# Transformer block on one core: regrouping the score-maximum pairs in the projection stage

## The chip, the core and the metric

The kernel runs on one core of a Trainium2 chip. A core has a matrix engine (TensorE, PE in the profile; PEld is its weight load), a vector engine (VectorE, DVE), a scalar engine (ScalarE, ACT), a general engine (GpSimd, POOL) and a queue engine that issues most DMAs (SyncE, SP). Each engine runs its own instructions in the order of the program and waits on semaphores for the others. Matmuls write to PSUM, which VectorE and ScalarE read; everything else lies in SBUF, on chip, or in DRAM.

The metric is device time in microseconds (us) of one launch; lower is better.

## The reference

One transformer block over 2048 tokens of width 640, in float32:

```
h   = x + softmax(q k^T / sqrt(20)) v  @ wo,   q, k, v = layernorm(x) @ wqkv,  32 heads of 20
out = h + (silu(z @ w_gate) * (z @ w_up)) @ w_down,   z = layernorm(h),  1728 hidden columns
```

The softmax subtracts the largest score of each query row. So that row maximum has to be known before the exponentials of the row, and the kernel computes scores twice: once for the maxima, and once for the exponentials.

## The kernel before

The launch has three stages: the projections (layer norm and q, k, v), the attention, and the feed-forward part with the output projection. The change lies in the first.

**Tiling.** The 2048 tokens are four chunks of 512 (`NC`, index c), each of four tiles of 128 (index t). The 32 heads are eight groups of four (`NG`, index g). A unit u = 4g + c is the scores of one group for one chunk of queries. Numbers are split into a high and a low part and multiplied in three products, so a projection block is 15 matmuls: 5 slices of the 640 columns times 3.

**Slots.** The stage is a list of 18 slots per chunk, 72 in all, numbered by `slot[0]`. In chunk 0 they are one slot with two blocks, an empty one, eight slots of a block each (slots 2 to 9), then eight of values. In chunks 1 and 2 there are five key blocks, five query blocks (`query_key`, line 435) and eight values (`value`, line 509: a tile of 128 tokens in two halves of 320 columns). Chunk 3 has the keys, the values, then the queries. The order of emission is the order on each engine.

**What a block leaves behind.** `keep` (lines 468 to 503) empties a block's PSUM tile through ScalarE and VectorE (before slot 8) or ScalarE and GpSimd (after), and for keys of chunks 0 and 1 adds the difference of the two halves of the chunk. The pieces go to DRAM arrays `q_d` and `k_d`, issued by ScalarE one block later (`store`, line 426). The first slots also split the weights into two parts, a slice or more per slot (`split_w`), out of `raw` tiles that the DMA has filled.

**PSUM.** `ps_wide` is a ring of three tiles of two banks, `ps_one` a ring of two tiles of one bank. A block's result lies in half a `ps_wide` tile in early slots and in `ps_one` later. Pairs use `ps_wide`.

**Pairs.** Between the projection matmuls, TensorE computes some of the scores whose row maxima the softmax needs. A pair is two matmuls for one tile of 128 queries against one chunk of 512 keys, two heads at once. There are two kinds:

- `max_pair` (lines 171 to 180) multiplies with the keys themselves; one VectorE reduction over 2 x 512 follows (line 180). It reads `keys[0]` and `queries[0]`, that is, the first unit's operands that the attention stage uses too, loaded by `load_keys` and `load_queries`.
- `max_halves` (lines 183 to 198) multiplies with differences and second halves of the keys. ScalarE writes the positive part of one half (line 193), then VectorE adds the other half and takes the maximum, once per head (line 195). It reads staged operands.

**Staging.** An item is one set of keys or queries for a group and a chunk, loaded into one of four `raw` buffers by four DMAs of SP (`stack`, line 148). The same four buffers hold the weights before. `load_items` loads the next item once its data is stored by plan (`stored_at`) and the pairs that used its buffer are all emitted. `ready` lets a pair go when its two items were loaded two slots earlier or more. This is the planner's count of slots; if a load in fact lands later, TensorE waits for it.

**Lists.** `urgent` holds the first unit's plain pairs with their earliest slots, `early` the staged pairs in a fixed order. `visit(n)` tries to load items and emits up to n pairs, from `urgent` first. It is called inside a block (after 9 of its 15 matmuls, except in chunk 0) with 3, inside a value from slot 10 on with 2, and at the end of each slot with 3 after a block and 2 after a value. The pairs that one visit emits are called a run here.

```
if n == 9 and slot[0] > 9:
    visit(2)
```

All the pairs of this stage are fixed in number; the attention stage computes the remaining maxima.

Of the kernel before, what the change touches and what calls it, by code (L numbers as in the profile page):

```python
# [26 lines left out]
NC = S // CH  # L27
# [3 lines left out]
NG = H // G  # L31
# [13 lines left out]
def tile_block(ctx: ExitStack, tc: tile.TileContext, x, wqkv, wo, wg, wu, wd, out):  # L45
# [27 lines left out]
    def ps_wide():  # L73
        return psum.tile([P, 2, CH], F32, name="ps_wide", tag="ps_wide", bufs=3)

    def ps_one():
        return psum.tile([P, CH], F32, name="ps_one", tag="ps_one", bufs=2)
# [104 lines left out]
    def max_halves(mx, q, k, pair, t, kc):  # L182


        ps = ps_wide()
        for b in range(2):
            rows = slice(b * ROW, b * ROW + NPART)
            nc.tensor.matmul(  # L188
                ps[:, b, :], q[rows, pair, t * P : (t + 1) * P], k[rows, pair, :],
                start=True, stop=True,  # L190
            )
        over = evp.tile([P, 2, CH // 2], F32, name="over", bufs=3)
        nc.scalar.activation(over, ps[:, :, CH // 2 :], AF.Relu)  # L193
        for b in range(2):
            nc.vector.tensor_tensor_reduce(  # L195
                over[:, b], ps[:, b, : CH // 2], over[:, b], 1.0, LOWEST, ALU.add, ALU.max,
                mx[:, b, pair, t, kc : kc + 1],
            )
# [44 lines left out]
    def moved(u, kc):  # L243
        return [t for t in range(TPC) if in_projections(u, kc, t)]
# [23 lines left out]
    with tc.tile_pool(name="pa", bufs=2) as pa:  # L268
# [18 lines left out]
        slot = [0]  # L287
        items, users = [], {}
# [23 lines left out]
        def staged_keys(g, c, kc, k, q):  # L312
            def one(t, pair):
                max_halves(mxs[g * NC + c], items[q][3], items[k][3], pair, t, kc)
                for n in (k, q):
                    users[n] -= 1
                load_items()

            def ready():
                return all(items[n][3] is not None and slot[0] >= items[n][4] + 2 for n in (k, q))  # L320

            pairs = [(t, pair) for t in moved(g * NC + c, kc) for pair in range(2)]
            for n in (k, q):
                users[n] += len(pairs)
            return [(ready, lambda a=a: one(*a)) for a in pairs]

        def unit_keys(u, kc, t, pair):
            max_pair(mxs[u], queries[u], keys[0], pair, t, kc, kc * CH)
            if u == 0 and (kc, t, pair) == (NC - 1, TPC - 1, 1):
                max_all(0)  # L330

        def in_unit(u, kc, at):
            return [
                (lambda: at <= slot[0], lambda t=t, pair=pair: unit_keys(u, kc, t, pair))
                for t in moved(u, kc) for pair in range(2)
            ]

        def staged(g, *sets):

            found = {}  # L340
            for c, kc in sets:
                for which, chunk in ((1, kc), (0, c)):
                    if (which, chunk) not in found:
                        found[which, chunk] = len(items)
                        users[len(items)] = 0
                        items.append([which, g, chunk, None, None])
            return [
                a for c, kc in sets for a in staged_keys(g, c, kc, found[1, kc], found[0, c])
            ]

        urgent = [a for kc in range(NC) for a in in_unit(0, kc, 18 * kc + 7)]
        early = [a for g in range(1, NG) for a in staged(g, (0, 0))]
        early += staged(1, (0, 1)) + staged(2, (0, 1))
        early += [a for g in range(3) for a in staged(g, (1, 1), (1, 0))]
        early += [a for g in range(3, NG) for a in staged(g, (0, 1), (1, 1), (1, 0))]
        early += staged(0, (2, 1), (2, 0))
# [1 line left out]
        def visit(n):  # L358
            load_items()
            for _ in range(n):  # L360
                for queue in (urgent, early):
                    if queue and queue[0][0]():
                        queue.pop(0)[1]()
                        break
# [64 lines left out]
        def query_key(c, m):  # L429

            z_hi, z_lo = zs[c]
            ps = ps_wide()[:, 0, :] if slot[0] < 7 else ps_one()
            for n, (a, w) in enumerate(((z_hi, w_hi), (z_lo, w_hi), (z_hi, w_lo))):
                for k in range(ND):
                    nc.tensor.matmul(  # L435
                        ps, w[:, k, m * P : (m + 1) * P], a[:, k, :],
                        start=(n == 0 and k == 0), stop=(n == 2 and k == ND - 1),
                    )
                    if n == 1 and k == 3 and c:
                        visit(3)  # L440
            keep(c, m, ps)
# [59 lines left out]
        def value(c, t, half):  # L501
            z_hi, z_lo = zs[c]
            ev = evs[t % 2]
            ps = ps_one()[:, :HALF]
            cs = slice(2 * D + half * HALF, 2 * D + (half + 1) * HALF)
            n = 0
            for a, w in ((z_hi, w_hi), (z_hi, w_lo), (z_lo, w_hi)):
                for k in range(ND):
                    nc.tensor.matmul(  # L509
                        ps, a[:, k, t * P : (t + 1) * P], w[:, k, cs],  # L510
                        start=(n == 0), stop=(n == 3 * ND - 1),
                    )
                    n += 1
                    if n == 9 and slot[0] > 9:
                        visit(2)
            dst = ev[:, half * 4 : half * 4 + 4, : G * VW].rearrange("p g (h w) -> p g h w", h=G)
            nc.scalar.activation(
                dst[:, :, :, :DH], ps.rearrange("p (g h d) -> p g h d", g=4, h=G), AF.Copy
            )
            if half == 1:  # L520
                rows = slice((c * TPC + t) * P, (c * TPC + t + 1) * P)
                store((v_d[rows], ev))
            else:
                store()
# [32 lines left out]
        for c in range(NC):  # L557
            lns = []
            work = (some_keys + some_queries if c else first) + parts
            if c == NC - 1:  # L560
                work = some_keys + parts + some_queries

                es[:] = [e for e in es if e is not third]
                es.insert(1, pa.tile([P, ND, CH], F32R, name="z_hi")[:, :2])
            for j, (kind, *which) in enumerate(work):
                slot[0] = 18 * c + j
                if c == 0 and j < 9:
                    for i in range(split_at[j], split_at[j + 1]):
                        split_w(i + 2)
                        if i % 2 == 1 and loaded < 8:  # L570
                            load_w(loaded)
                            loaded += 1
                if j == 0 and c + 1 < NC:
                    if c > 0:
                        load_x(c + 1)
                    lns = norm(c + 1)
                if which:
                    if (c, j) == (0, 0):
                        first_blocks((0, 1), (1, 0), (1, 1), (0, 2), (1, 2))
                        for m, ps in enumerate(firsts):  # L580
                            keep(0, m, ps)
                    else:
                        (query_key if kind == "block" else value)(c, *which)
                visit(2 if kind == "value" else 3)
                finish_keep()
                if c == 0 and j == 6:
                    for ev in evs:
                        nc.gpsimd.memset(ev, 1.0)
                if j == (4 if c == 0 else 3):
                    load_keys(0, slice(c * CH, (c + 1) * CH))  # L590
                if j == (4 if c == 0 else 8) and c < 3:
                    load_queries(c)
                if 0 in ends:
                    finish_at = min(finish_at, slot[0] + 2)
                    if slot[0] == finish_at:
                        max_finish(0)
                if j == 14 and c == 3:
                    load_values(0)
                for _ in range(2 if j >= 5 else 1):
                    if j >= 1 and lns:  # L600
                        lns.pop(0)()
                if c + 1 < NC and 0 <= j - flip_at[c] < ND:
                    flip(c + 1, j - flip_at[c])
                if c == NC - 1 and j == 11:
                    nc.scalar.activation(
                        pa.tile([P, 1], F32, name="exp_table"), eps_t, AF.Exp
                    )
# [418 lines left out]
    for u in range(NU):  # L1026
        g, c = divmod(u, NC)
# [3 lines left out]
        for kt in range(NT):  # L1031
# [51 lines left out]
            k = 2 * (u - NU + 8)  # L1083
# [574 lines left out]
```

## Time and profile before

| | |
|---|---|
| median of 3 runs | 2109.74 us (2107.43 to 2110.51) |
| the profiled execution | 2110.45 us, span 2108.7 us |
| TensorE busy | 2066.6 us, 98% of the span |
| VectorE, ScalarE, GpSimd busy | 79%, 69%, 33% |
| projections | 0 to about 389.5 us of the span |
| attention | about 389.5 to 1980 us |

The span runs from the first to the last instruction. A line of the timeline gives the start and the duration in us, the engine, the line of the kernel, the operation, what it writes and reads, the shape, and how many like it were merged; in brackets the idle time before it and what ended that. In a line of windows stand the stretch, its length, the busy time of TensorE, weight loads, VectorE, ScalarE and GpSimd with their instruction counts, the granted TensorE clock as a share of full speed, the DMA engines' share, and GB/s. A group's line has its busy time and the mean duration of one in ns, then the idle time before. A matmul's end is modelled, so starts tell more than durations.

### The profile page before, as it was taken

The page shows a single profiled execution, that of the slowest core. Times are in us where ns is not written, and L with a number is a line of the kernel's source. Part 1 is how long each engine was busy: PE and PEld are TensorE (multiplying, and loading weights), DVE is VectorE, ACT ScalarE, POOL GpSimd, SP SyncE. Part 2 cuts the span into 40 slices and gives each one's busy share as a digit, 9 for nine tenths or more (in the row PEclk, how much of TensorE's full clock was granted, in tenths as well). Part 3 has the DMA queues.
Part 4 walks back from the last instruction along what each step waited for, and adds up shares of the span by engine and source line. Part 5 has one row for each costly group of instructions (what it writes and reads, how often), then busy time and mean ns, then how long its engine had stood idle before and what let it go on. Part 6 is the DMA issues. An engine that isn't in the chain of part 4 may idle for free.

```text
span 2108.7 us, 37142 instructions
## 1 busy us (share of the span) xinstructions
PE 2066.6 (98%) x12636; PEld 1207.3 (57%) x12636; DVE 1659.5 (79%) x3631; ACT 1445.4 (69%) x2835; POOL 691.2 (33%) x949
## 2 busy tenths in 40 slices
PE   7999999999999999999999999999999999999998
PEld 5656566433333433334333433335578888888888
DVE  6767867788888888888888988886368766666677
ACT  3647575899999999999999999996743222212221
POOL 2231110233443424353420001001135434653555
PEclk9999999999999999999999999999999999999999
DMA  8565544335263443543631213131137755884642
GB/s 257 174 205 179 164 140 127 87 116 153 88 183 103 148 140 118 156 139 133 188 111 56 52 32 94 34 115 61 35 121 266 263 169 188 298 301 159 196 152 94
DMA packets 197285, 305.38 MB, mean 145 GB/s; under 512 B 47440, under 2 KB 82256, under 8 KB 196072
## 3 DMA queue, kind: packets, MB, share of 16 engines
q1 hardware_dynamic: 183512, 274.15, 41.2%
q10 hardware_dynamic: 13584, 28.85, 4.6%
q8 instruction: 102, 1.67, 0.4%
q14 instruction: 87, 0.71, 0.1%
HBM read 203.82 MB, written 98.30 MB: 143 GB/s over the span
## 4 chain that ended last, share of the span: by engine, by line
PE 87%; DVE 6%; DMA 3%; issue 2%; ACT 1%; ACTq 1%; POOL 0%; SPq 0%; DVEq 0%; POOLq 0%
PE acc L960 24%; PE ps_one L950 15%; PE ps_a L1121 15%; PE ps_max L204 12%; PE ps_b L1215 8%; PE ps_one L509 3%; PE ps_wide L188 3%; PE ps_one L435 3%; DVE over L195 2%; PE ps_max L688 2%; DVE mx L180 2%; PE ps_b L688 1%; DMA halves<-j_d 1%; ACTq L426 1%; ACT over L193 0%
## 5 line engine op out<-in xcount | busy, mean ns | idle before, releaser
L956 ACT ACTIVATE probs<-ps_one 128x512 f32<-128x512 f32 x2048 | 1056.9, 616 | 66.1 <-PE ps_one L950 41.3
L210 DVE TENSOR_REDUCE mx<-ps_max 128x1 f32<-128x512 f32 x1472 | 925.6, 683 | 109.3 <-PE ps_one L950 77.6
L950 PE MATMUL ps_one<-q_stk,k_stk 62*128 62x512 f32 x2048 | 586.4, 451 | 2.6 <-DVE m L86 1.7
L960 PE MATMUL acc<-probs,v_stk 128*32 128x512 f32 x4096 | 547.2, 607 | 0.0
L950 PEld LDWEIGHTS ps_one<-q_stk,k_stk 62*128 62x128 f32 x2048 | 251.6, 184 | 432.9 <-ACT probs L956 397.1
L204 PE MATMUL ps_max<-k_stk,q_stk 60*128 60x512 f32 x1472 | 381.7, 425 | 1.4 <-DVE mx L210 1.3
L204 PEld LDWEIGHTS ps_max<-k_stk,q_stk 60*128 60x128 f32 x1472 | 271.9, 186 | 26.6 <-DVE mx L210 2.7
L195 DVE CUSTOM_DVE_ANT_0 over<-ps_wide,over 128x256 f32<-128x256 f32 x512 | 184.7, 420 | 82.9 <-ACT over L193 82.8
L1336 DVE TENSOR_TENSOR tmp<-ps_a,tmp 128x512 f32<-128x512 f32 x208 | 141.2, 689 | 119.9 <-PE ps_a L1121 94.1
L193 ACT ACTIVATE over<-ps_wide 128x512 f32<-128x512 f32 x256 | 138.6, 597 | 76.9 <-PE ps_wide L188 32.2
L1215 PE MATMUL ps_b<-halves,yp 128*128 128x320 f32 x1032 | 179.3, 308 | 2.0 <-DMA halves<-j_d 1.2
L960 PEld LDWEIGHTS acc<-probs,v_stk 128*32 128x32 f32 x4096 | 80.7, 108 | 175.3 <-issue 166.7
L1215 PEld LDWEIGHTS ps_b<-halves,yp 128*128 128x128 f32 x1032 | 165.1, 188 | 18.6 <-POOL yp L86 1.5
L995 POOL TENSOR_TENSOR o<-o,rb 128x512 f32<-128x512 f32 x31 | 39.9, 1286 | 411.2 <-DMA q_stk<-q_d 178.8
L1121 PE MATMUL ps_a<-t,units 128*128 128x512 f32 x624 | 162.6, 396 | 0.0
L1121 PE MATMUL ps_a<-z,units 128*128 128x512 f32 x516 | 133.9, 394 | 0.0
L1121 PEld LDWEIGHTS ps_a<-t,units 128*128 128x128 f32 x624 | 112.6, 188 | 18.8 <-ACT tmp L1349 0.2
L86 POOL TENSOR_TENSOR yp<-y,yp 128x256 fp32r<-128x256 f32 x96 | 60.2, 627 | 188.3 <-ACT yp L85 188.3
L188 PE MATMUL ps_wide<-raw 60*128 60x512 f32 x512 | 107.6, 468 | 12.3 <-DVE mx L195 7.1
L1220 DVE TENSOR_TENSOR h<-ps_b,h 128x320 f32<-128x320 f32 x248 | 109.9, 480 | 6.9 <-PE ps_b L1215 5.4
L1121 PEld LDWEIGHTS ps_a<-z,units 128*128 128x128 f32 x516 | 93.1, 187 | 15.9
L85 ACT ACTIVATE yp<-tmp 128x512 fp32r<-128x512 f32 x40 | 25.3, 632 | 103.1 <-POOL tmp L1208 103.1
(189 smaller groups left out, 2195.5 us busy)
## 6 DMA issues: line engine op xcount, KB each, us to landing
units<-w_d SPq DMA_DIRECT2D x186, 256.0 KB
w_d<-stage SPq DMA_DIRECT2D x106, 256.0 KB
halves<-j_d SPq DMA_DIRECT2D x70, 320.0 KB
j_d<-stage SPq DMA_DIRECT2D x42, 320.0 KB
k_stk<-k_d SPq DMA_DIRECT2D x64, 160.0 KB
q_stk<-q_d SPq DMA_DIRECT2D x64, 160.0 KB
raw<-k_d SPq DMA_DIRECT2D x54, 160.0 KB
rb<-r_d SPq DMA_DIRECT2D x32, 256.0 KB
```

Of the source, the lines that this page charges most:

```text
L188: nc.tensor.matmul(ps[:, b, :], q[rows, pair, t * P : (t + 1) * P], k[rows, pair, :], start=True, stop=True,)
L193: nc.scalar.activation(over, ps[:, :, CH // 2 :], AF.Relu)
L195: nc.vector.tensor_tensor_reduce(over[:, b], ps[:, b, : CH // 2], over[:, b], 1.0, LOWEST, ALU.add, ALU.max, mx[:, b, pair, t, kc : kc + 1],)
L204: nc.tensor.matmul(ps, queries[u][rows, pair, t * P : (t + 1) * P], keys[u // NC][rows, pair, kc * CH : (kc + 1) * CH], start=True, stop=True,
L210: nc.vector.tensor_reduce(mxs[u][:, b, pair, t, kc : kc + 1], ps, axis=AX.X, op=ALU.max)
L950: nc.tensor.matmul(ps, keys[u // NC][rows, p, kt * P : (kt + 1) * P], queries[u][rows, p, :], start=True, stop=True,)
L956: nc.scalar.activation(probs[p][:, b, :], ps, AF.Exp, scale=scale)
L960: nc.tensor.matmul(acc[32 * j : 32 * j + 32, :], values[u // NC][:, kt, j * VW : j * VW + 32], probs[j // 2][:, j % 2, :], start=(kt == 0) ...
L1121: nc.tensor.matmul(ps.rearrange("p (t n) -> p t n", t=TPC), w[k][:, i], z[k][:, :, j], start=(first and m == 0), stop=(last and m == len(n ...
L1215: nc.tensor.matmul(ps, a, b, start=(n == 0), stop=(n == len(pairs) - 1))
L1220: nc.vector.tensor_tensor(out=h, in0=ps, in1=h, op=ALU.add)
L1336: add = lambda out, ps, x: nc.vector.tensor_tensor(out=out, in0=ps, in1=x, op=ALU.add)
```

## The change

There are three edits, all in the projection stage.

Visits: inside a value, only the second half of a tile (the odd value slot) still has a visit of 2 pairs; the visit at the end of a value slot is of 3 instead of 2. Two value slots thus hold runs of 3, 2 and 3 pairs instead of 2, 2, 2 and 2.

First unit: its pairs against key chunks 0 and 1 leave `urgent` (and with it `max_pair`) and go to the front of their places in `early`, so they are done by `max_halves` with staged operands. This makes 272 staged pairs and 16 plain ones out of 256 and 32, and 54 items out of 50. The first two items are now loaded in slot 4, ahead of the loads of `keys[0]` and `queries[0]` in that slot. Before slot 24, `ready` asks for three slots since the load instead of two.

Wide tiles: a block's result lies in `ps_wide` up to slot 4 instead of slot 6; slots 5 and 6 now use `ps_one`.

```
             def ready():
-                return all(items[n][3] is not None and slot[0] >= items[n][4] + 2 for n in (k, q))
+                return all(items[n][3] is not None and slot[0] >= items[n][4] + 2 + (slot[0] < 24) for n in (k, q))
...
-        urgent = [a for kc in range(NC) for a in in_unit(0, kc, 18 * kc + 7)]
-        early = [a for g in range(1, NG) for a in staged(g, (0, 0))]
-        early += staged(1, (0, 1)) + staged(2, (0, 1))
+        urgent = [a for kc in (2, 3) for a in in_unit(0, kc, 18 * kc + 7)]
+        early = [a for g in range(NG) for a in staged(g, (0, 0))]
+        early += [a for g in range(3) for a in staged(g, (0, 1))]
...
-            ps = ps_wide()[:, 0, :] if slot[0] < 7 else ps_one()
+            ps = ps_wide()[:, 0, :] if slot[0] < 5 else ps_one()
...
-                    if n == 9 and slot[0] > 9:
+                    if n == 9 and half and slot[0] > 9:
                         visit(2)
...
-                visit(2 if kind == "value" else 3)
+                visit(3)
```

## The prediction

> **What bounds the kernel now.** I read the page first, then busy time by stage, then TensorE's waits in the stage that the change touches, then the order of instructions there.
>
> ```profile
> span 2108.7 us, 37142 instructions
> PE 2066.6 (98%) x12636; PEld 1207.3 (57%) x12636; DVE 1659.5 (79%) x3631; ACT 1445.4 (69%) x2835; POOL 691.2 (33%) x949
> ```
> ```profile
> 0.00:389.50 389.50, 361.29 (x1773) 247.42 (x1773) 281.22 (x1210) 228.01 (x420) 79.29 (x66) 0.98 0.58 175
> 48.40:55.20 6.80, 6.33 (x15) 4.74 (x16) 5.45 (x10) 2.38 (x4) 2.10 (x3) 0.50 0.96 293
> 120.10:126.90 6.80, 5.95 (x17) 3.58 (x17) 2.15 (x12) 2.17 (x4) 1.74 (x2) 0.50 0.63 212
> ```
>
> TensorE (first column after the length, then weight loads, VectorE, ScalarE, GpSimd, clock, DMA share) is busy throughout; the edit lies wholly in the projections, which the first stretch holds, and leaves the rest of the kernel alone, so I assume that what the projections save or lose goes through to the end. There TensorE has 389.5 - 361.3 = 28.2 us without a matmul, and its busy time also holds hidden costs: switches between kinds of matmul, and 2 x 6.8 us at half clock (0.50 in the last two rows). Those three are all that can be won; the number of matmuls does not change.
>
> **Part 1: fewer runs among the values.** A run is a few pairs of score matmuls (L188 or L176) between projection matmuls (L509 values, L435 blocks). Its price shows in the starts:
>
> ```profile
> 279.06 0.73 PE L188 MATMUL ps_wide<-raw 60*128 60x512 f32 x4
> 279.72 0.42 PE L509 MATMUL ps_one<-w_lo,z_hi 128*128 128x320 f32 x1
> 279.97 0.89 PE L509 MATMUL ps_one<-w_hi,z_lo 128*128 128x320 f32 x5
> 280.80 0.85 PE L188 MATMUL ps_wide<-raw 60*128 60x512 f32 x4
> 281.58 0.66 PE L405 MATMUL ps_one<-ident,xt 128*128 128x128 f32 x4
> ```
> ```profile
> 195.46 1.08 PE L435 MATMUL ps_one<-z_lo,w_hi 128*128 128x512 f32 x4
> 196.47 0.96 PE L188 MATMUL ps_wide<-raw 60*128 60x512 f32 x6
> 197.37 0.50 PE L435 MATMUL ps_one<-z_lo,w_hi 128*128 128x512 f32 x1
> ...
> 198.95 0.85 PE L188 MATMUL ps_wide<-raw 60*128 60x512 f32 x4
> 200.00 0.50 PE L188 MATMUL ps_wide<-raw 60*128 60x512 f32 x2 [0.19 <-DVE mx L195]
> 200.43 1.43 PE L435 MATMUL ps_one<-z_hi,w_hi 128*128 128x512 f32 x5
> ```
> ```profile
> 131.36 1.30 PE L435 MATMUL ps_one<-z_hi,w_hi 128*128 128x512 f32 x5
> 132.50 1.30 PE L435 MATMUL ps_one<-z_lo,w_hi 128*128 128x512 f32 x5
> ```
>
> Two pairs take 279.72 - 279.06 = 0.66 us and three 197.37 - 196.47 = 0.90, so a pair is 0.24 and a run adds 0.66 - 0.48 = 0.18 of its own. Undisturbed, five block matmuls take 132.50 - 131.36 = 1.14; the six between two runs take 198.95 - 197.37 = 1.58 where 6/5 x 1.14 = 1.37 would do: 0.21 more for leaving and coming back. A run removed saves about 0.18 + 0.21 = 0.39 us.
>
> Followed slot by slot, the two lists hold the same 288 pairs before and after, in 119 and 106 runs: among the values 64 runs become 48 (two slots had four runs of 2, and get 3, then 2 and 3), among the blocks 55 become 58. That is 16 x 0.39 = 6.2 saved, and 3 x 0.39 = 1.2 lost.
>
> Against it stands PSUM. There are three wide tiles. The run at 196.47 filled all three, and its third came back for the pair at 200.00, 3.53 us after the run's start. VectorE's reductions follow each other at 0.35 us, two to a pair:
>
> ```profile
> 268.63 0.42 DVE L195 CUSTOM_DVE_ANT_0 over<-ps_wide,over 128x256 f32<-128x256 f32 x1 [0.25 <-ACT over L193]
> 268.98 0.08 DVE L195 DVE_READ_ACCUMULATOR2_ANT mx<- 128x1 f32 x1
> 268.98 0.42 DVE L195 CUSTOM_DVE_ANT_0 over<-ps_wide,over 128x256 f32<-128x256 f32 x1
> ```
>
> So tiles come back 0.70 apart, the first two at about 2.13 and 2.83. After the change, the run of 3 that ends an odd value slot starts 0.66 + 1.08 = 1.74 us after the run of 2 inside it (279.06 to 280.80). Its second pair, due at 1.98, waits for the first tile of the run of 2 until 2.13; its third, then due at 2.37, waits until 2.83: 0.61 us in all. The run of 3 after a whole value finds its tiles free. Before, two end runs pay 281.58 - 280.80 - 0.66 = 0.12 each. So a pair of slots nets 0.39 - (0.61 - 0.24) = 0.02 by this pessimistic count, and 0.39 if the tiles return in time. I take 0.2, between the two, because VectorE's return times were read where it also had other work: 16 x 0.2 = **3 us saved**, ends 0.3 and 6.2. Blocks: **1.2 lost**, ends 0 and 1.2.
>
> [...]
>
> **Part 2: three slots' notice before slot 24.** The longest stall after the start is a load that arrives late in slot 21:
>
> ```profile
> 115.99 1.07 PE L435 MATMUL ps_one<-z_lo,w_hi 128*128 128x512 f32 x4
> 118.45 0.46 PE L188 MATMUL ps_wide<-raw 60*128 60x512 f32 x1 [1.39 <-DMA raw<-q_d]
> 120.95 1.61 PE L188 MATMUL ps_wide<-raw 60*128 60x512 f32 x5 [2.04 <-DMA raw<-q_d]
> 122.50 0.79 PE L435 MATMUL ps_one<-z_lo,w_hi 128*128 128x512 f32 x1
> 123.09 2.33 PE L435 MATMUL ps_one<-z_hi,w_lo 128*128 128x512 f32 x5
> 125.36 1.65 PE L188 MATMUL ps_wide<-raw 60*128 60x512 f32 x6
> ```
>
> Four matmuls take 1.01 (195.46 to 196.47), so the run was due at 117.00: 1.45 late. The run then takes 122.50 - 118.45 = 4.05 instead of 0.90, and the six matmuls after it 2.86 instead of 1.58 (197.37 to 198.95), since the clock is at 0.50 from 120.10. Together 1.45 + 3.15 + 1.28 = 5.9 us. The pairs that waited (group 7) were loaded in slot 19; in the new lists they are loaded in slot 19 too, but used from slot 22. Slot 20 keeps 6 pairs, so this is one slot of at least 4.4 us more against 3.5 us of waiting: **5.9 saved**.
>
> Late next: first unit's key differences for chunk 1, loaded in slot 22, used in slot 24, and group 1's, loaded in 23, used in 25. SP issues them behind the key load of slot 21. The late load's own history sets the margin: issue from 113.21 for 3.10 us (below), last landing 120.95, some 4.6 us after the last issue. Two slots are about 10.7 us, two loads of the kind need 7 to 11. I book **1 lost**, ends 0 and 5.9.
>
> **Part 3: first unit's chunks 0 and 1.** 16 pairs leave the plain reduction for the halved one:
>
> ```profile
> L193 ACT ACTIVATE over<-ps_wide 128x512 f32<-128x512 f32 x256 | 138.6, 597 | 76.9 <-PE ps_wide L188 32.2
> ```
> ```profile
> 142.76 1.01 PE L176 MATMUL ps_wide<-k_stk,q_stk 60*128 60x512 f32 x4
> 144.41 0.49 PE L176 MATMUL ps_wide<-k_stk,q_stk 60*128 60x512 f32 x2 [0.63 <-DVE mx L180]
> 144.83 1.43 PE L435 MATMUL ps_one<-z_hi,w_hi 128*128 128x512 f32 x5
> ```
>
> ScalarE gains 16 x 0.597 = 9.6 us, inside its 389.5 - 228.0 = 161 us of idle. TensorE's part is equal. A run of 3 plain pairs took 144.83 - 142.76 = 2.07 against 1.48 for halved ones (198.95 to 200.43): 0.6. In chunk 1 about two runs are so: **1.2 saved**, ends 0 and 1.8. Four more loads (54 for 50) give 16 more issues on SP; it idles between them, unless loads pile up as below.
>
> **Part 4: the start, slots 4 to 9.** The part I know least.
>
> ```profile
> 37.25 0.74 ACT L85 ACTIVATE w_hi<-raw 128x640 fp32r<-128x640 f32 x1 [3.49 <-DMA k_stk<-k_d]
> 43.09 0.77 PE L176 MATMUL ps_wide<-k_stk,q_stk 60*128 60x512 f32 x2
> 45.66 0.51 PE L176 MATMUL ps_wide<-k_stk,q_stk 60*128 60x512 f32 x2 [1.81 <-DVE v_stk L86]
> 48.87 0.80 PE L176 MATMUL ps_wide<-k_stk,q_stk 60*128 60x512 f32 x2 [2.70 <-DVE e L476]
> 49.59 2.50 PE L435 MATMUL ps_one<-z_hi,w_hi 128*128 128x512 f32 x5
> 55.85 0.97 PE L176 MATMUL ps_wide<-k_stk,q_stk 60*128 60x512 f32 x6
> ```
> ```profile
> 45.03 3.84 SPq L148 DMA_DIRECT2D raw<-q_d  x4
> 113.21 3.10 SPq L148 DMA_DIRECT2D raw<-q_d  x4
> ```
>
> Now the slot-7 pairs wait for slots 5 and 6 to be emptied from wide tiles: 49.59 - 43.09 = 6.50 instead of 0.90, 5.6 lost; and slot 8's block runs at half clock. With the change slots 5 and 6 go to the two ps_one tiles. The pairs find wide tiles free, but slot 7's own block now needs slot 5's tile, which VectorE released just before 45.66; so the same emptying is waited for earlier. And the pairs need two staged loads. The second reuses the weight buffer whose last split (slot 5) freed the query load at 45.03; it lands about 45.03 + 3.84 + 4.6 = 53.5. Should nothing move earlier, the three pairs start at 53.5 instead of ending by 49.59: 53.5 + 0.9 - 49.6 = 4.8 lost. What moves earlier: ScalarE stood 3.49 us behind the landing of the first unit's key load. That load and the query load now go behind the staged ones, so evacuation and splits may run 3.5 us sooner, or more; then 1.3 is lost, and the half clock, which costs slot 8 55.85 - 49.59 - 3.4 = 2.9, may go. So -4.5 to +4.8; I take **0**, the middle. Behind SP's waiting load stand the key, query and group 1 loads; group 1's pairs in slot 9 wait for the latter. That cost lies within the range.
>
> [...]
>
> **Sum.** -3 + 1.2 - 5.9 + 1 - 1.2 + 0 = -7.9 us. The profiled execution took 2110.45 us (span 2108.7), 0.7 above the median 2109.74: 2110.45 - 7.9 = 2102.6, or 2102 against the median.
>
> **Rivals.**
> *The start gets clean*: ScalarE, free of the key load's landing, empties early, no half clock: 4.5 better, 2097.5. For it: the 3.49 us row. Against it: two loads must land where none was waited for.
> [...]
> *The late load only moves* to slots 24 and 25, half clock included: 5.9 instead of 1, 2107.5.
> *Slower: first unit's staged load holds the start.* SP is in order; if stores of ScalarE must wait for the key and query loads stuck behind the 45.03 load, as they waited 3.49 us before, evacuation of slots 6 to 8 stops until they land. Two more batches of four at 3.1 to 3.8 us plus 4.6 after 48.87 give 60 to 61, against 49.59: 11 lost there, and 4.8 more as group 1's load slips likewise: 2102.5 + 15 = 2118. It decides once slot 8 starts 12 us late. For it: the 3.49 row shows the coupling; against: that row's load goes.
>
> **How the numbers follow.** Forecast 0.52, clean start 0.19: faster 0.71. Full PSUM 0.08 and moved load 0.08 end within 0.2% (4.2 us, about what a measurement of this kernel tells from no change): same 0.16. Held start: slower 0.13. Range 2094 to 2110: from a clean start with part of the larger run saving to the two that end level; the held start is left out.
>
> **What would show it.** Right: values' runs at 48, no DMA wait before 118 to 121, clock 0.50 there gone, L176 x32 instead of x64. Wrong: a gap over 4 us before the first L188, a wait on raw near 130, third pairs at over 0.6 us of wait, or a change after 389 us that isn't the shift.

## The result, and the profile after

| | median | range | runs |
|---|---|---|---|
| before | 2108.98 us | 2106.56 to 2112.41 | 12 |
| after | 2109.83 us | 2106.14 to 2114.71 | 12 |

The ratio of after to before is 1.0005, with a 95% interval of 0.9996 to 1.0014: no difference that these runs can tell. The forecast was 2102 us and faster. The profiled execution of after took 2110.56 us. Its page and its projections:

```profile
PE 2063.7 (98%) x12636; PEld 1209.8 (57%) x12636; DVE 1652.8 (78%) x3679; ACT 1451.7 (69%) x2851; POOL 691.3 (33%) x949
```
```profile
0.00:391.90 391.90, 358.58 (x1773) 247.77 (x1773) 275.43 (x1258) 234.50 (x435) 79.25 (x66) 0.99 0.58 179
```

TensorE's busy time in the projections fell by 361.29 - 358.58 = 2.7 us, yet the projections end 2.4 us later, so TensorE stands idle 5.1 us longer. I cut the stage at the first matmul of each kind of work (B: blocks, V: values; the number is the chunk). Windows of after, columns as before (length, busy time of TensorE and the others, clock, DMA share):

```profile
22.95:65.34 42.39, 33.89 (x141) 25.20 (x139) 27.58 (x81) 18.93 (x36) 7.10 (x8) 0.95 0.83 250
65.34:101.34 36.00, 35.44 (x203) 27.18 (x203) 23.77 (x120) 26.42 (x50) 7.75 (x6) 0.92 0.53 163
...
326.67:363.24 36.57, 32.75 (x188) 23.76 (x186) 26.96 (x107) 17.67 (x37) 1.28 (x1) 1.00 0.38 116
```

| stage | before | after | b4 (below) |
|---|---|---|---|
| B0, from the first block | 38.68 | 42.39 | 35.81 |
| V0 | 36.46 | 36.00 | 33.57 |
| B1 | 60.74 | 59.91 | 56.11 |
| V1 | 35.73 | 34.94 | 34.70 |
| B2 | 64.42 | 63.94 | 62.25 |
| V2 | 35.98 | 36.30 | 34.30 |
| keys of chunk 3 | 31.20 | 30.24 | 30.08 |
| V3 | 34.22 | 36.57 | 33.51 |
| queries of chunk 3 | 29.51 | 28.69 | 28.35 |
| sum | 366.94 | 368.98 | 348.68 |

Each column is one execution. The start lost 3.7 us, V3 lost 2.4, and everything else gained 4.0 together, half of what was forecast. The first block starts within 1.9 us of the same time in all kernels here; I compare sums from there. TensorE's waits in the projections, first of before, then of after (engine, what it waited to do, for whom; us in total, times, longest):

```profile
PE ps_wide L188 <- DVE mx L195: 7.1, 24, 0.9
PE ps_wide L188 <- DMA raw<-q_d: 3.4, 2, 2.0
```
```profile
PE ps_wide L188 <- DVE mx L195: 11.4, 40, 1.2
PE ps_wide L188 <- DMA raw<-q_d: 7.5, 7, 2.6
PE ps_one L435 <- DVE v_stk L86: 2.3, 1, 2.3
```

The load wait at 118 to 121 us is gone, as forecast. In its place come a start that waits for loads and pairs that wait for wide tiles. The prediction's signs of being wrong show as well: waits for a wide tile reach 1.2 us (it named 0.6 for third pairs), and a staged load is waited for 0.8 us at 137.79 (it named 130). The start first (TensorE's timeline of after, then SP's):

```profile
46.57 0.47 PE L188 MATMUL ps_wide<-raw 60*128 60x512 f32 x1 [0.42 <-DMA raw<-q_d]
49.60 0.93 PE L188 MATMUL ps_wide<-raw 60*128 60x512 f32 x5 [2.56 <-DMA raw<-q_d]
50.46 2.21 PE L435 MATMUL ps_one<-z_hi,w_hi 128*128 128x512 f32 x5
...
60.21 0.73 PE L188 MATMUL ps_wide<-raw 60*128 60x512 f32 x4
63.31 0.47 PE L188 MATMUL ps_wide<-raw 60*128 60x512 f32 x1 [2.36 <-DMA raw<-q_d]
64.64 0.76 PE L188 MATMUL ps_wide<-raw 60*128 60x512 f32 x1 [0.87 <-DMA raw<-q_d]
65.34 1.70 PE L509 MATMUL ps_one<-w_hi,z_hi 128*128 128x320 f32 x5
```
```profile
41.79 3.66 SPq L148 DMA_DIRECT2D raw<-q_d  x4
45.55 2.38 SPq L148 DMA_DIRECT2D k_stk<-k_d  x4
49.48 4.15 SPq L148 DMA_DIRECT2D q_stk<-q_d  x4
53.73 4.28 SPq L148 DMA_DIRECT2D raw<-k_d  x4
58.11 3.88 SPq L148 DMA_DIRECT2D raw<-q_d  x4
```

Slot 8's block starts at 50.46, 0.9 us later than before. The loss is one slot further on: group 1's queries, wanted at 60.9, are issued from 58.11 only, behind two loads (45.55 and 49.48) that in this kernel nothing reads before slot 43. Behind the wait the granted clock is 0.50 from 64.48 to 71.30, so the clock of V0 reads 0.92.

### The profile page after: what moved, and what is told of

The parts are those of the page before. It is cut to its first block, busy times and chain, and to the rows that moved or that the text cites. A ratio compares the mean times of both kernels' runs of the same rounds, so it can differ in the third digit from the quotient of the medians.

```text
span 2108.8 us, 37276 instructions
## 1 busy us (share of the span) xinstructions
PE 2063.7 (98%) x12636; PEld 1209.8 (57%) x12636; DVE 1652.8 (78%) x3679; ACT 1451.7 (69%) x2851; POOL 691.3 (33%) x949
## 4 chain that ended last, share of the span: by engine, by line
PE 84%; DMA 4%; DVE 4%; issue 3%; ACT 1%; POOL 1%; SPq 1%; ACTq 0%; POOLq 0%; DVEq 0%
PE acc L960 24%; PE ps_one L950 15%; PE ps_a L1121 15%; PE ps_max L204 12%; PE ps_b L1215 8%; DVE over L195 2%; PE ps_one L509 2%; PE ps_one L435 2%; PE ps_max L688 2%; PE ps_wide L188 2%; PE ps_b L688 1%; DMA halves<-j_d 1%; ACT over L193 1%; DMA raw<-k_d 1%; DMA k_d<-v_stk 1%
## 5 line engine op out<-in xcount | busy, mean ns | idle before, releaser
L195 DVE CUSTOM_DVE_ANT_0 over<-ps_wide,over 128x256 f32<-128x256 f32 x544 | 195.3, 420 | 97.9 <-ACT over L193 97.8
L193 ACT ACTIVATE over<-ps_wide 128x512 f32<-128x512 f32 x272 | 145.8, 598 | 73.2 <-PE ps_wide L188 31.3
L1215 PEld LDWEIGHTS ps_b<-halves,yp 128*128 128x128 f32 x1032 | 165.2, 188 | 18.4 <-POOL yp L86 1.5
L188 PE MATMUL ps_wide<-raw 60*128 60x512 f32 x544 | 111.3, 462 | 20.4 <-DVE mx L195 11.4
```

The costliest lines, as they stand in the source:

```text
L188: nc.tensor.matmul(ps[:, b, :], q[rows, pair, t * P : (t + 1) * P], k[rows, pair, :], start=True, stop=True,)
L195: nc.vector.tensor_tensor_reduce(over[:, b], ps[:, b, : CH // 2], over[:, b], 1.0, LOWEST, ALU.add, ALU.max, mx[:, b, pair, t, kc : kc + 1],)
L1215: nc.tensor.matmul(ps, a, b, start=(n == 0), stop=(n == len(pairs) - 1))
```

## Experiments

All ratios below are to runs of before on the same chip, with 95% intervals. The stage lengths and their sums are from one profiled execution each. They differ by up to 2.0 us between kernels that run the same code there (B0 is 42.39 in after and 40.39 in `a3_unit`), and a profiled execution can lie some us off its kernel's median (`a1_notice` 4.0 below; `a5_runs_notice`, `b1_late` and `b2_pool` 4.2, 5.2 and 5.4 above). So they show where time goes, and the ratios decide how much. First I took the change apart.

**One: the notice alone** (`a1_notice`).

```diff
-  return all(... slot[0] >= items[n][4] + 2 for n in (k, q))
+  return all(... slot[0] >= items[n][4] + 2 + (slot[0] < 24) for n in (k, q))
```

> The kernel before with one edit: before slot 24 a unit's pairs become ready three slots after its loads were issued instead of two. Theory 1 (each gain is real and the new start eats them): the load wait and the half clock at 118 to 121 us go, the projections end at 383 to 385 us instead of 389.5, the time falls by 4 to 6 us. Theory 2 (the late load and the half clock only move to another place): half a clock for at least 3.4 us at a new place in the projections, their end within 1.5 us of 389.5, the time unchanged. Theory 3 (what the projections save is lost again behind them): the projections end near 384 and the time is still unchanged.

Measured: 2109.04 us, ratio 1.0004 (0.9995 to 1.0013). The sum from the first block is 365.63, only 1.3 below before. No load was waited for at 118, but there was a stall in the same slot, with half a clock behind it. Timeline of all engines, then two windows:

```profile
112.09 2.53 ACTq L426 DMA_DIRECT2D k_d<-e  x3
114.75 1.57 ACT L193 ACTIVATE over<-ps_wide 128x512 f32<-128x512 f32 x3 [3.66 <-DMA k_d<-e]
115.38 0.42 DVE L195 CUSTOM_DVE_ANT_0 over<-ps_wide,over 128x256 f32<-128x256 f32 x1 [4.12 <-ACT over L193]
116.30 0.50 PE L188 MATMUL ps_wide<-raw 60*128 60x512 f32 x2 [2.11 <-DVE mx L195]
```
```profile
111.54:114.96 3.42, 2.66 (x11) 1.66 (x11) 0.00 (x0) 0.21 (x1) 0.35 (x1) 1.00 0.83 276
114.96:118.37 3.41, 1.88 (x8) 1.24 (x9) 2.96 (x15) 3.18 (x6) 1.24 (x1) 1.00 0.77 257
118.37:121.79 3.42, 3.42 (x10) 2.65 (x9) 2.54 (x12) 1.34 (x2) 1.33 (x2) 0.50 0.62 170
```

Read it from the top: ScalarE issues three stores of keys and stands 2.53 us at them. It evicts the wide tiles (L193) only behind them, at 114.75. VectorE waits 4.12 us for that, and TensorE 2.11 us for a free tile. None of my theories had this wait; theory 2 is nearest.

**Two: the runs alone** (`a2_runs`).

```diff
-                    if n == 9 and slot[0] > 9:
+                    if n == 9 and half and slot[0] > 9:
...
-                visit(2 if kind == "value" else 3)
+                visit(3)
```

> The kernel before with the two edits on runs alone: three pairs instead of two in a run behind a value slot, and no run inside an unsplit half. Theory 1: 13 to 16 runs fewer by some 0.39 us each, less the wide-tile waits of the third pairs: projections end 2 to 4 us earlier than 389.5, time 2 to 4 us lower, the wait and the half clock near 120 us still there (perhaps a slot away). Theory 2 (the third pair of each run waits for its PSUM tile and takes the gain): stages of values as long as before within 0.5 us each, time within 1 us. If the first value slots of a chunk lose time to ScalarE, which stands at its own k_d and q_d stores, chunk 3's values are about 2 us longer here too.

Measured: 2108.68 us, ratio 0.9999 (0.9988 to 1.0011). Sum 365.71, 1.2 below before. V0, V1 and V2 are 1.1, 0.2 and 0.3 shorter, V3 is 36.23, 2.0 longer, as the third sentence said. TensorE still waits 2.5 us for loads between 108 and 130 us, with half a clock for 3.4 us from 119.67.

**Three: everything but the runs** (`a3_unit`: the changed kernel without the second experiment's edit).

> The changed kernel with the runs among values as before: three slots' notice, the first unit staged with the key differences, wide tiles for five slots only. Theory 1: the stage to slot 10 is about 4 us longer than before's 61.3 us with a half clock near 64 us, the wait at 118 to 121 is gone, so projections end at 388 to 391 us and the time is within 2 us of before. Theory 2: the same start, and a new load wait with half a clock behind slot 21: projections end at 393 us or later, time 2 to 4 us above before.

Measured: 2110.22 us, ratio 1.0007 (0.9996 to 1.0019). First value at 64.09 and half a clock from 64.96 to 68.38, as in after; B0 40.39, sum 370.53. The projections end at 394.23, as theory 2 has it, though no wait for a staged load is over 1.9 us. The four stages of values take 143.26 us here and 143.81 in after: in the changed kernel the larger runs gave nothing.

**Four: notice and runs, old start** (`a5_runs_notice`: experiments one and two together).

> The changed kernel with the first unit and the wide tiles as before: fewer, larger runs among values and the three slots' notice. Theory 1: start as before (first value at 61.3 us), no half clock between 65 and 200 us, projections end at 381 to 386 us, time 4 to 8 us lower: the start alone is what the changed kernel loses by. Theory 2: the larger runs wait where the smaller did not and the load wait moves: projections end at 388 to 391 us, time within 2 us of before. Theory 3: projections end near 384 us and the time does not follow.

Measured: 2106.92 us, ratio 0.9994 (0.9985 to 1.0004). The start is before's, first value at 60.12, but the sum is 368.28: V3 took 38.00 us, and half a clock stands at 117.81 and at 332.86. So the old start doesn't bring the forecast gain back, and theory 1 falls as well. The same stall as in the first experiment stands at both places. In after it can be seen at the start of V3, on ScalarE and on TensorE:

```profile
325.94 2.57 ACTq L426 DMA_DIRECT2D k_d<-e  x3
328.63 1.57 ACT L193 ACTIVATE over<-ps_wide 128x512 f32<-128x512 f32 x3 [2.15 <-DMA k_d<-e]
```
```profile
326.11 0.62 PE L188 MATMUL ps_wide<-raw 60*128 60x512 f32 x3
...
330.18 0.50 PE L188 MATMUL ps_wide<-raw 60*128 60x512 f32 x2 [1.05 <-DVE mx L195]
```

A run of three fills all three tiles; while ScalarE stands at its stores, 2.57 us here, none comes back. The new theory: ScalarE's stores hold the projections, in both kernels (the hold, below). SP's rows in the projections after 60 us hint at the coupling of the two queues. In after:

```profile
SPq L148 <- DMA v_d<-ev: 16.0, 5, 5.8
SPq L148 <- DMA q_d<-e: 10.5, 5, 3.5
...
SPq L148 <- DMA k_d<-e: 9.0, 8, 3.2
```

SP's loads at line 148 read `q_d` and `k_d`, yet wait 16.0 us for the landing of stores to `v_d`, which they don't read. The instructions in the trace of after name a completion semaphore for each transfer: the 1587 transfers of SP and the 109 of ScalarE name the same eight. In each of the five waits of these 16.0 us (5.8, 5.2, 0.4, 0.4 and 4.3), the semaphore waited for is the one that SP's next issue names. It goes the other way too: in before, ScalarE's stores of keys at 116.92 and 118.04 are issued 0.02 us after the landings of SP's loads `raw<-k_d` and `raw<-q_d` that had the same semaphores. So here a load of SP waited for the landing of a store of ScalarE, and a store for that of a load. Two edits follow: other loads at the start, and another engine for the stores.

**Five: the two unread loads later** (`b1_late`).

```diff
-                if j == (4 if c == 0 else 3):
+                if j == (11 if c == 0 else 3):
                     load_keys(0, slice(c * CH, (c + 1) * CH))
-                if j == (4 if c == 0 else 8) and c < 3:
+                if j == (12 if c == 0 else 8) and c < 3:
                     load_queries(c)
```

> The changed kernel with the loads of chunk 0's k_stk and q_stk, which nothing reads before slot 43 now, issued behind slots 11 and 12 instead of slot 4. If group 1's query load is late in slot 9 because it queues behind them on SP, the matrix unit's wait for raw at 61 to 65 us is gone, the first value starts at 60.5 to 62 us instead of 65.3, there is no half clock near 64 us, and the projections end 3 to 5 us earlier. If the load is late for another cause (the stores it reads, or the buffers), the first value stays at 64 to 66 us.

Measured: 2114.12 us, ratio 1.0027 (1.0014 to 1.0040). The first value starts at 62.09, 39.20 after the first block, against 42.39 in after; the wait in slot 9 and the half clock at 64 are gone. The cause of that wait is settled. But V0 takes 45.01 us, and the kernel is slower than before. The next loads are late again. Little of that is the moved loads' own issue (3.1 us on SP, from 81.89); most of it is SP waiting for stores of `v_d`, before the moved loads and within the issue at 88.96 (SP's waits from 62.09 to 107.10, then SP's and TensorE's timeline):

```profile
SPq L148 <- DMA v_d<-ev: 11.4, 2, 6.2
```
```profile
88.96 7.52 SPq L148 DMA_DIRECT2D raw<-q_d  x4
```
```profile
95.09 0.46 PE L188 MATMUL ps_wide<-raw 60*128 60x512 f32 x1 [2.57 <-DMA raw<-q_d]
99.25 1.61 PE L188 MATMUL ps_wide<-raw 60*128 60x512 f32 x5 [3.71 <-DMA raw<-q_d]
```

**Six: GpSimd issues the stores of the changed kernel** (`b2_pool`).

```diff
-        def store(*last, queue=nc.scalar):
+        def store(*last, queue=nc.gpsimd):
...
-            store(*pieces, queue=nc.sync if (c, m) == (NC - 1, 2 * ND - 1) else nc.scalar)
+            store(*pieces, queue=nc.sync if (c, m) == (NC - 1, 2 * ND - 1) else nc.gpsimd)
```

> The changed kernel with the stores of k_d, q_d and v_d in the projections issued by GpSimd instead of ScalarE. If ScalarE, held at its own stores, holds the evictions of the wide tiles and with them the matrix unit, then the matrix unit's waits of ps_wide for mx (11.4 us, 40 of them) fall to 2 to 5 us, chunk 3's values return from 36.6 to about 34.5 us, and the projections end 4 to 8 us earlier, unless GpSimd, which splits the blocks, is late with its splits then. If the third pair's own place in PSUM makes those waits, they stay at 10 to 12 us and the projections end within 1.5 us of before.

Measured: 2095.96 us, ratio 0.9949 (0.9930 to 0.9968). Waits of TensorE, then of SP, in the projections:

```profile
PE ps_wide L188 <- DMA raw<-q_d: 7.7, 5, 3.6
PE ps_wide L188 <- DVE mx L195: 5.6, 29, 0.3
```
```profile
SPq L148 <- DMA k_d<-e: 4.3, 1, 4.3
```

The waits for wide tiles halve and none is over 0.3 us; SP no longer waits for `v_d` at all; V3 is 33.50. What is left of load waits, 7.7 us, lies mainly at the start, which is as long as in after (42.05). A store keeps GpSimd busy for 0.51 to 0.69 us; that is hidden (GpSimd is busy 133 of the 349 us in b4's stages).

**Seven: both** (`b4_pool_late`: edits five and six in the changed kernel).

> Both edits together (chunk 0's k_stk and q_stk loaded behind slots 11 and 12, stores issued by GpSimd). If the start and ScalarE's stores are two separate losses, their gains add: projections end at 380 to 385 us, time 7 to 11 us below the changed kernel's. If one stall only covers the other, the gain is that of the better of the two alone.

Measured: 2090.17 us against 2108.53 of before on that chip, ratio 0.9918 (0.9903 to 0.9933). This beats both kernels. The projections end at 371.17, and their sum is 20.3 us below after's, where edit six alone took off 8.9 and edit five alone added 10.3 (by the ratios about 18 and 12 us off and 5 added). So the two don't add: the late loads that cost V0 so much beside ScalarE's stores cost nothing here. In the rows shown SP issues four transfers in 1.5 and 2.3 us, where after took 2.4 to 4.3. SP's start, and TensorE's waits:

```profile
41.02 2.28 SPq L148 DMA_DIRECT2D raw<-q_d  x4
46.67 1.48 SPq L148 DMA_DIRECT2D raw<-k_d  x4
```
```profile
PE ps_wide L188 <- DVE mx L195: 5.6, 29, 0.3
...
PE ps_wide L188 <- DMA raw<-q_d: 1.6, 3, 0.8
```

**Eight: notice, runs, old start, GpSimd's stores** (`b5_runs_pool`: experiment four with edit six).

> The kernel before with fewer, larger runs among values, three slots' notice, and the stores issued by GpSimd; first unit and start as before. If ScalarE's k_d store is what stands behind the load wait at 111 to 117 us, the gap of 2 to 3 us there and the half clock behind it are gone, and the projections end at 380 to 385 us. If the half clock comes at a fixed 71.7 us after the first one whatever the gaps, it stays at 117 to 120 us.

Measured: 2094.30 us, ratio 0.9939 (0.9924 to 0.9953). Sum 350.85, and at full clock from 50.30 to the end of the stage: here neither the gap nor the half clock at 118 comes. In before it had begun 71.7 us after the first one (48.43 and 120.11); here the first one comes too, and none begins 71.7 us later.

**Nine: the kernel before with GpSimd's stores, none of the change** (`c1_before_pool`).

> The kernel before with one edit: GpSimd issues the stores of k_d, q_d and v_d in the projections. If ScalarE's stores held the matrix unit in the kernel before as in the changed one, and the change's own edits come to little, this kernel is 10 to 14 us below before (2095 to 2099, projections end at 375 to 380 us) although none of the change is in it. If ScalarE's hold matters only where the changed kernel's larger runs meet it, the time falls by less than 5 us.

Measured: 2096.22 us, ratio 0.9935 (0.9921 to 0.9948), sum 354.06. So the stores cost the kernel before as much, 12.9 us in the trace. The late load at 118 that Part 2 of the prediction was about is gone too, without any notice. Before issued its keys from 109.72 and its queries from 113.21; here:

```profile
105.71 2.39 SPq L148 DMA_DIRECT2D raw<-k_d  x4
108.20 2.14 SPq L148 DMA_DIRECT2D raw<-q_d  x4
```

With this base I could weigh the change's parts free of the hold.

**Ten: b4 without the larger runs** (`c2_no_runs`).

> The changed kernel with GpSimd's stores and chunk 0's k_stk and q_stk loaded late, but the runs among values as before. With the hold gone the larger runs should save what was worked out for them, 3 us between 0.3 and 6.2: so this kernel ends its projections 1 to 5 us later than the 371.2 us of the same kernel with larger runs, in the four stages of values (33.6, 34.7, 34.4 and 33.5 us there). Under the rival, that the third pair of a run waits for its PSUM tile and eats the gain whoever stores, the stages of values are within 0.3 us each of those.

Measured: 2094.86 us, ratio 0.9935 (0.9917 to 0.9953); the interval overlaps b4's. Sum 350.72, 2.0 above b4's 348.68. V0 to V3 were 35.04, 34.23, 35.13 and 33.18, 1.5 longer together.

**Eleven: b4 with two slots' notice** (`c3_no_notice`).

> The changed kernel with GpSimd's stores and late loads of chunk 0's k_stk and q_stk, but two slots' notice throughout. If the notice is worth what was worked out for it, a wait for raw of 3 to 4 us comes back near slots 20 to 22 with a half clock behind it, and the projections end 4 to 6 us later than 371.2. If loads are late only because their issue was held by the semaphores that SP shared with ScalarE's stores, they land within two slots now and the projections end within 1.5 us of 371.2.

Measured: 2107.67 us, ratio 0.9992 (0.9982 to 1.0002). Neither expectation: nothing came back near slot 21, but the start took 52.38 us instead of 35.81, with waits of 5.30, 3.66, 3.55 and 1.93 us for staged queries between 45 and 69 us. The notice is what makes the new start possible; it isn't a gain on its own.

**Twelve: b4 with wide tiles for seven slots** (`c4_wide7`).

> The changed kernel with GpSimd's stores and late loads of chunk 0's k_stk and q_stk, but wide tiles for the first seven slots. The wait of slot 7's block for the tile of slot 5's (2.0 us) goes; if nothing else takes its place the first value starts at 56 to 57.5 us instead of 58.3 and the projections end 1 to 2 us earlier. If that wait only hides ScalarE's or VectorE's lag, the start is as long as with five.

Measured: 2094.73 us, ratio 0.9931 (0.9915 to 0.9946), overlapping b4's. The wait of slot 7's block goes, but the start takes 37.81 us, 2.0 more than b4's: the first pairs wait 2.24 us for a wide tile that VectorE has yet to empty, then 2.00 for a load. As the prediction had it, the same emptying is waited for at one place or the other. The sum is 354.47, so 3.8 us more are lost behind the start, where this edit changes nothing; why is open.

Two things were still open: whether it is ScalarE that should not issue, or SP that waits, and whether the notice by itself is worth anything.

**Thirteen: SP issues the stores of the changed kernel** (`b3_sync`: as in experiment six, with `nc.sync`).

> The changed kernel with the projections' stores issued by SP instead of ScalarE; loads, start and runs as changed. Two things can be behind the gain of GpSimd's stores. If it is ScalarE alone, which no longer stands at its stores when a wide tile is to be evicted, this kernel gains the same 12 to 14 us (2095 to 2098; waits of ps_wide for mx near 5.6 us). If it is SP, whose loads waited for the landing of stores, the stores in its own order hold the loads as much or more: the waits for mx fall to about 6 us, the waits for raw stay at 7 us or grow, and the time stays within 3 us of the changed kernel or above it.

Measured: 2097.79 us, ratio 0.9948 (0.9933 to 0.9962); TensorE no longer waits for any staged load, though SP itself waits 34.2 us for GpSimd's splits before its stores. The waits for wide tiles are 7.3 us, above the 5.6 expected. Here SP's loads stand between stores in one queue, and the gain is that of GpSimd's stores (0.9949), so that alone isn't the loss. The loss is with ScalarE as issuer. Whether all of it is ScalarE's own standing, or part of it loads that came late because ScalarE's store was late, these runs don't separate: without ScalarE's stores both go.

**Fourteen: notice alone on the kernel of experiment nine** (`d1_notice_pool`).

> The kernel before with GpSimd's stores and the three slots' notice. Without the notice the same kernel took 0.9935 of before and its matrix unit waited 0.4 us for raw. If the late load at 118 us was itself made by ScalarE's stores, the notice has nothing left to save: ratio within 0.002 of 0.9935, projections end within 1.5 us of 377.1 us. If the notice is worth its 4 to 6 us whoever stores, the projections end at 371 to 373 us.

Measured: 2096.36 us, ratio 0.9943 (0.9930 to 0.9955); sum 353.97 against 354.06. The notice saves nothing once ScalarE doesn't store.

## Why the prediction was wrong

**What bounds.** That the projections' gain goes through to the end held: b4's stages are 366.94 - 348.68 = 18.3 us shorter, its time 18.4 us. But the view was incomplete. The gaps were counted on TensorE alone; the waits of ScalarE and SP, which show who held the tiles and the loads, weren't read by cause.

**Part 2 is the first step that failed:** "one slot of at least 4.4 us more against 3.5 us of waiting: 5.9 saved", with 1 us for what is late next. By itself the notice moved the sum by -1.3 us, where -4.9 was booked, and the time not at all (experiment one). Behind the late load stood ScalarE's store of keys in the same slot: the same place, the same half clock, another releaser. Before's trace has both, the store and what made the load late (ScalarE's and SP's timelines, then a row of SP's waits from 28 to 130 us):

```profile
115.12 3.23 ACTq L426 DMA_DIRECT2D k_d<-e  x3
```
```profile
109.72 3.44 SPq L148 DMA_DIRECT2D raw<-k_d  x4
```
```profile
SPq L148 <- DMA v_d<-ev: 5.0, 1, 5.0
```

ScalarE stands 3.23 us at its stores, to 118.35; TensorE waits for the load from 117.06. And the load was late because SP stood from 104.66 to 109.66 for the landing of a store of `v_d` by ScalarE; without ScalarE's stores that wait and the late load are gone (experiments nine and fourteen). I asked what is late next among loads only, and not among the engines that free the tiles.

**Part 1 failed too: the price was right, its cover wasn't.** A run of three behind a run of two:

```profile
175.61 0.73 PE L188 MATMUL ps_wide<-raw 60*128 60x512 f32 x4
...
177.35 0.88 PE L188 MATMUL ps_wide<-raw 60*128 60x512 f32 x4
178.43 0.50 PE L188 MATMUL ps_wide<-raw 60*128 60x512 f32 x2 [0.19 <-DVE mx L195]
178.86 0.66 PE L405 MATMUL ps_one<-ident,xt 128*128 128x128 f32 x4
```

It takes 178.86 - 177.35 = 1.51 instead of 0.90: 0.61, the number of the prediction. Free of the hold the values went from 139.47 to 136.58 us (`d1_notice_pool` to `b5_runs_pool`), 2.9 saved where 3 was forecast, and the blocks lost 0.0 of the 1.2. But experiment ten has 1.5 for the same edit, the ratios tell neither from nothing (0.9943 and 0.9939, 0.9935 and 0.9918, with overlapping intervals), and a price of 0.61 goes with the prediction's pessimistic end of 0.3. So that 2.9 lies so near to 3 may be luck. With ScalarE's stores the same edit gave 141.89 to 144.68 (`a1_notice` to `a5_runs_notice`), 2.8 lost, all in V3, and 0.5 lost in the changed kernel. The working took ScalarE as free because it idles 161 us; a run of three needs it free just then: the run of two before it started 1.74 us earlier (175.61 to 177.35).

**Part 3.** The plain pairs' matmuls went from 64 to 32, as said. No run isolates the 1.2 us. The four more loads weren't free: the staged pairs at the start wait 0.42 and 2.56 us for theirs, which belongs to Part 4.

**Part 4: 0 booked, +3.7 measured** (+1.7 in `a3_unit`, with the same start), within its ends of -4.5 and +4.8; half a clock (0.50, 64.48 to 71.30) then stands over the start of V0. The better end isn't worked out there: 1.3 lost less 2.9 for the half clock is -1.6, and no row gives the rest. The pieces came as written: ScalarE's row that stood at 37.25 starts at 35.22, slot 7's block waits 2.3 us for slot 5's tile, and the first staged pairs wait until 49.60. The sentence on group 1's load, "that cost lies within the range", was the part that happened: 2.36 and 0.87 us of waiting, behind loads that nothing reads soon (experiment five).

**The sum.** Forecast -7.9. In the trace of after: +3.7 at the start, -1.7 in all later stages, where -7.9 had been expected: +2.0. The times say +0.9, within what they can tell. Of the 9.9 us between, the start makes 3.7, the stages of values 4.4 (+1.4 instead of -3, by V3's 2.4) and the other blocks 1.8.

**The hold isn't the whole account.** It slows both kernels, by about as much. Where neither has ScalarE's stores, the change still gains nothing: before is at 0.9935 and 0.9943 (experiments nine and fourteen), the changed kernel at 0.9949 and 0.9948 (six and thirteen), and its start is 42.05 and 39.15 us against 36.38 and 36.84. Only with the start mended as well does it come to 0.9918, with a sum 5.4 us below that of experiment nine, and even that interval overlaps with 0.9935's. Against experiment nine's kernel, the changed one in experiments six and thirteen saves 2.0 and 1.8 us in the values and loses 5.7 and 2.8 in the start and 4.0 and 1.0 in B1. So what the start loses eats what the runs save, and no run shows the forecast 7.9 us as the change's own.

**Rivals.** "The late load only moves" came nearest in time (2107.5), though what moved was the holder and not the load. "Full PSUM" (0.08) has its sign in after, where TensorE's waits for wide tiles rose from 7.1 to 11.4 us. But no run shows VectorE's pace eating the gain of the runs: with GpSimd's stores TensorE waits 5.6 us in the same runs, never over 0.3. The held start did not come about: slot 8 started 0.9 us late, not 12. Its coupling, stores against loads, was right, and was the key to the whole case; I had read the 3.49 us row and confined it to the start.

## What to carry to other kernels

An engine that evicts PSUM shouldn't also issue stores that may have to wait: its share of idle time (161 of 389.5 us for ScalarE in before) says nothing about whether it is free when a tile is needed (it stood 3.23 us at three stores there). When a wait is taken away, look in the same slot for the next releaser on every engine, and not only for the next of the same kind; two waits that lie on top of each other show as one. Before pricing an edit, list the waits of the issuing queues by cause: in this case loads that waited 16.0 us for the landing of stores that they don't read were the sign of completion semaphores that two queues shared.

## What was not expected of the hardware

**Who issues a store.** Moving the stores from ScalarE to GpSimd was worth 0.65% of the kernel before (ratio 0.9935), more than anything in the change, though the same stores are made. ScalarE stood 2.53 us at three stores in experiment one and 2.57 in after, and TensorE then waited 2.11 and 1.05 us for a wide tile. GpSimd spent 0.51 to 0.69 us on a store in experiment six, and no wait of L188 for a wide tile was over 0.3 us there.

**When the half clock comes.** In the projections of before and after the granted clock is 1.00 or 0.50 and changes by steps of 3.413 us. From the start of the first full-clock record, stretches at 1.00 and 0.50 last by turns 37.55, 6.83, 64.85 and 6.83 us in before (11, 2, 19 and 2 steps; half clock from 48.43 and 120.11) and 37.55, 3.41, 10.24 and 6.83 us in after (11, 1, 3 and 2; half clock from 50.82 and 64.48). Three steps of after:

```profile
57.65:61.06 3.41, 3.29 (x16) 2.14 (x14) 2.67 (x13) 2.90 (x5) 0.92 (x1) 1.00 0.73 232
61.06:64.48 3.42, 0.47 (x1) 0.18 (x1) 2.67 (x8) 1.08 (x2) 0.90 (x1) 1.00 0.73 187
64.48:67.89 3.41, 3.25 (x10) 2.84 (x11) 2.31 (x9) 1.11 (x2) 1.25 (x1) 0.50 0.82 250
```

The step ahead of this half clock has 0.47 us of matmuls. Ahead of the other in after it is 1.22 us, ahead of the two in before 0.51 and 0.82, and in the first experiment 1.88 of 3.41 us; the step with 2.66 us there was followed by full clock. So a half clock came once behind a step with 1.53 us without matmuls, and in after none came behind the step from 40.59 to 44.00, which has 1.83 us without (1.58 of matmuls). What decides between these wasn't shown.
